# Linear attention ahead of two expert layers: output in natural layout with 128 moving columns, column-tiled own weights, scores last in a unit

## The chip, the cores and the metric

The program runs on one core of a Trainium2 chip, in one launch. The metric is the device time of one execution in microseconds (us), lower is better. The engines are called TensorE (PE; its weight loads are PEld), VectorE (DVE), ScalarE (ACT), GpSimd (POOL) and SyncE (SP, which issues most DMAs). Every engine executes its own instructions strictly in the order in which the program lists them.

## The reference

Three steps, each on the result of the one before, with 4 batches, 8 heads, 768 tokens and 48 numbers to a head (so 3072 rows of 384):

```python
for t in range(S):                       # attention, per batch and head
    cur = np.einsum('bhd,bhe->bhde', u[None] * kt, vt)
    y[:, :, t] = np.einsum('bhd,bhde->bhe', rt, state + cur)
    state = wt[:, :, :, None] * state + np.einsum('bhd,bhe->bhde', kt, vt)
# MoE 1: each row goes to the expert with the largest of 8 logits:
#   out = softmax weight * sigmoid(x @ w_output_gate)[e] * (relu(x @ w1[e]) @ w2[e])
# MoE 2: noisy logits, the two best experts of 8, weighted by a softmax over the two
```

## The kernel before

**Units.** The attention is cut into NU = 24 units: 128 tokens of one batch with all 8 heads, taken as 4 pairs of heads (HP = 4). Unit i is chunk i // 4 of batch i % 4, so the state that leaves unit i is needed by unit i + 4. Most tiles of a unit have 112 partitions (two heads of 48 at partitions 0 and 64) by 4 pairs by 128 tokens.

**What a unit needs.** `prep` (VectorE) clamps the decays w, scans them backwards to `g` and forwards to `cp`, and multiplies to `ke` = k*g and `R` = r*cp. `scores` (TensorE) multiplies ke with R into two PSUM banks; ScalarE copies them to `at` and GpSimd masks them (two `affine_select`). `keys` turns ke over, `kv` forms the unit's sum of outer products, `kv_add` (VectorE) adds the `carry` of the batch to `s0`, `carry_on` multiplies that by the next unit's whole decay, `advance` copies it to the block-diagonal `state`. `yout` adds, in one PSUM bank, state times R and v times at, with the heads' numbers on the partitions; ScalarE copies that out (`yT`), `ynat` turns it to natural layout (tokens on the partitions). The own term (r·u·k)v goes beside that: `ruk` forms p = r*k*u from a load of its own (GpSimd, two instructions), `bonus` sums it by head (VectorE, `s`) and multiplies v by it (GpSimd, `sv`). `rows_out` adds both to `x` and stores the 128 rows to `xrow` in memory. `xt` turns x over once more, `logits` multiplies it with the gates, and a `Route1` object does the routing of MoE 1: `choose` (8 small VectorE instructions), `rank` (TensorE), `place` (9 small VectorE instructions), `enter` (GpSimd scatters of 128 table entries).

**Order.** All queues are written by hand: the loop `for i in range(NU + 1)` lists for each engine the prep of unit i + 2, the scores of i, the kv and yout of i - 1, the ynat and x of i - 2 and the logits of i - 3. The routing is done in 12 groups of two units (`GROUPS`). Loads run three to four units ahead.

**Behind it.** When the rows are stored and routed, each expert's rows are gathered from `xrow`, and the two expert layers follow. `early` starts the first expert's work as filler before the last units are routed. PSUM has eight banks, and each name of `banks` is bound to one or two of them.

The own term passes from GpSimd to VectorE and back (p comes from `ruk`):

```python
s = wk.tile([C, H], F32, name="s")
nc.vector.tensor_reduce(s, t["p"].rearrange("p (h d) -> p h d", h=H), AX.X, OP.add)
sv = t["sv"] = wk.tile([C, H, D], F32, name="sv", bufs=3)
nc.gpsimd.tensor_tensor(sv, t["v"].rearrange("p (h d) -> p h d", h=H), bc(s, D), OP.mult)
```

Of the kernel before, what the change touches and what calls it, by code (L numbers as in the profile page):

```python
# [21 lines left out]
C = 128  # L22
# [10 lines left out]
MID = 2  # L33
FA, FB = 3, 1
EG = 6
FILL = (0, 1, 0, 0, 2)
NT = N + 128
W_MIN, W_MAX = 0.625, 1.25
TS = 16
# [14 lines left out]
GROUPS = [(i, 2) for i in range(0, NU, 2)]  # L54
# [11 lines left out]
def rwkv_moe_kernel(ctx, tc, r, k, v, w, rT, kT, wT, rkv, u, g1, a1, a2, g2, noise, b1, b2, out):  # L66
# [4 lines left out]
    psum = ctx.enter_context(tc.tile_pool(name="psum", bufs=1, space=PSUM))  # L71
# [50 lines left out]
    def banks(**plan):  # L122

        turns = {n: itertools.cycle(b) for n, b in plan.items()}
        return lambda name: psum.tile([128, 512], F32, name="b" + next(turns[name]))
# [370 lines left out]
    with ExitStack() as c2:  # L496
        ac = c2.enter_context(tc.tile_pool(name="ac", bufs=1))
# [5 lines left out]
        NS = HP * (C + 1)  # L503

        def flat(x):
            return x.rearrange("p a b -> p (a b)")

        def load(i):
            t = T.setdefault(i, {})
            for nm, src in (("w", wT), ("k", kT), ("r", rT)):  # L510
                t[nm] = ld.tile([PP, HP, C], F32, name=nm + "T")
                nc.sync.dma_start(t[nm], src[i])

        def load_rows(i):
            t = T.setdefault(i, {})
            t["rk"] = ld.tile([C, 2, DM], F32, name="rk")
            nc.sync.dma_start(t["rk"], rkv[i, :, 0:2])
            t["v"] = ld.tile([C, DM], F32, name="v", bufs=5)
            nc.sync.dma_start(t["v"], rkv[i, :, 2])

        bank = banks(sp0="0", sp1="1", kp="23", pp="4", yp="5", xp="6", lp="7")

        def quads(t, n=128):
            return t[:, 0:HP * n].rearrange("p (a b) -> p a b", a=HP)
# [4 lines left out]
        nc.vector.memset(sind, 0.0)  # L529
        nc.vector.memset(sind[:, :, C:C + 1], 1.0)  # L530
        clamped, start = [], []
        for i in range(2):
            t = ac.tile([PP, NS + 1], F32, name=f"clamped{i}")
            nc.vector.memset(t[:, ::C + 1], 0.0)
            clamped.append(t)
# [6 lines left out]
        ub = ac.tile([C, DM], F32, name="ub")  # L542
        nc.sync.dma_start(ub, rows(u, 0, [[0, C], [1, DM]]))
# [5 lines left out]
        state, carry = [], []  # L549
        for b in range(B):  # L550
            t = ac.tile([PP, HP, PP], F32, name=f"state{b}")
            nc.gpsimd.memset(t, 0.0)
            state.append(t)
            carry.append(ac.tile([PP, HP, D], F32, name=f"carry{b}"))
# [43 lines left out]
        def prep(i):  # L598
            t = T[i]
            v = nc.vector  # L600
            wc = clamped[i % 2]
            v.tensor_scalar(wc[:, 1:NS + 1].rearrange("p (a b) -> p a b", a=HP)[:, :, 0:C], t["w"],
                            W_MIN, W_MAX, OP.max, OP.min)
            yield
            g = wk.tile([PP, HP, C + 1], F32, name="g")
            v.tensor_tensor_scan(flat(g)[:, ::-1], wc[:, NS:0:-1], flat(sind)[:, ::-1], 0.0, OP.mult, OP.add)
# [6 lines left out]
            we = t["we"] = wk.tile([PP, HP], F32, name="we", bufs=6)  # L613
            v.tensor_copy(we, g[:, :, 0])
# [4 lines left out]
            R = t["R"] = wk.tile([PP, HP, C], F32, name="R", bufs=4)  # L619
# [10 lines left out]
        def bonus(i):  # L630
            t = T[i]
            s = wk.tile([C, H], F32, name="s")
            nc.vector.tensor_reduce(s, t["p"].rearrange("p (h d) -> p h d", h=H), AX.X, OP.add)
            sv = t["sv"] = wk.tile([C, H, D], F32, name="sv", bufs=3)
            nc.gpsimd.tensor_tensor(sv, t["v"].rearrange("p (h d) -> p h d", h=H), bc(s, D), OP.mult)

        def guard(i):
            w = T[i]["w"]
# [18 lines left out]
        def keys(i):  # L657
            t = T[i]
            kp = quads(bank("kp"))
            for pr in range(HP):  # L660
                nc.tensor.transpose(kp[:, pr, 0:PP], t["ke"][:, pr, :], ident[:PP, :PP])
            t["kk"] = wk.tile([C, HP, PP], F32, name="kk")
            nc.scalar.copy(t["kk"], kp[:, :, 0:PP])

        def kv(i):
            t = T[i]
            if i < NU - B:
                pp = t["pp"] = quads(bank("pp")[:PP], D)
                for pr in range(HP):
                    for r0, r1, c0 in ((0, 64, 0), (64, PP, D)):  # L670
                        nc.tensor.matmul(pp[r0:r1, pr, :], t["kk"][:, pr, r0:r1],
                                         t["v"][:, pr * 96 + c0:pr * 96 + c0 + D], start=True, stop=True)

        def kv_add(i):
            t = T[i]
            if i < NU - B:
                t["s0"] = wk.tile([PP, HP, D], F32, name="s0", bufs=4)
                if i < B:
                    nc.scalar.copy(t["s0"], t["pp"])
                else:  # L680
                    nc.vector.tensor_tensor(t["s0"], t["pp"], carry[i % B], OP.add)

        def carry_on(i):
            if i < NU - B:
                nc.vector.tensor_tensor(carry[i % B], T[i]["s0"], bc(T[i + B]["we"], D), OP.mult)

        def advance(i):
            if i < NU - B:
                for r0, r1, c0 in ((0, 64, 0), (64, PP, 64)):
                    nc.scalar.copy(state[i % B][r0:r1, :, c0:c0 + D], carry[i % B][r0:r1])  # L690

        def yout(i, prs=range(HP)):
            t = T[i]
            c, b = divmod(i, B)
            if prs[0] == 0:
                t["yp"] = quads(bank("yp")[:PP])
            yp = t["yp"]
            for pr in prs:
                if c:
                    nc.tensor.matmul(yp[:, pr, :], state[b][:, pr, :], t["R"][:, pr, :], start=True, stop=False)  # L700
                for hh in range(2):
                    h = 2 * pr + hh
                    m = 64 if hh == 0 else D
                    nc.tensor.matmul(yp[64 * hh:64 * hh + m, pr, :], t["v"][:, h * D:h * D + m], t["at"][:, hh, pr, :],
                                     start=(c == 0), stop=True)
            if prs[-1] == HP - 1:
                t["yT"] = wk.tile([PP, HP, C], F32, name="yT")
                nc.scalar.copy(t["yT"], yp)

        def ynat(i):  # L710
            t = T[i]
            yn = t["yn"] = quads(bank("kp"))
            for pr in range(HP):
                nc.tensor.transpose(yn[:, pr, 0:PP], t["yT"][:, pr, :], ident[:PP, :PP])

        def rows_out(i):
# [3 lines left out]
            nc.vector.tensor_tensor(x.rearrange("p (h d) -> p h d", h=H),  # L720
                                    t["yn"].rearrange("p a (h d) -> p (a h) d", h=2)[:, :, 0:D], t["sv"], OP.add)
# [5 lines left out]
        def xt(i):  # L727
            t = T[i]
            xp = quads(bank("xp"))[:, 0:KD]
            for k in range(KD):  # L730
# [93 lines left out]
        for _ in prep(1):  # L824
            pass
# [619 lines left out]
```

## Time and profile before

| | us |
|---|---|
| three runs: lowest, median, highest | 984.24, 985.2, 986.06 |
| the profiled execution, and its span | 983.54, 982.0 |
| busy: TensorE, VectorE, ScalarE, GpSimd | 894.6, 570.9, 421.6, 485.8 |
| first and last store of x | 34.1, 241.9 |
| mean granted TensorE clock, as a share of full speed | 0.945 |

The span is what the trace covers. The attention fills the first quarter of it and the expert layers the rest, so the busy shares of the whole span mix stages with different limits.

### The profile page before, as it was taken

The numbers are of one execution on the slowest core, as the hardware profiler recorded it, in microseconds if no ns is written. First come the engines' busy times: TensorE is split into PE (matmuls) and PEld (weight loads), VectorE is DVE, ScalarE is ACT, GpSimd is POOL, SyncE is SP. The second block draws the span as 40 slices with busy tenths as digits, with TensorE's granted clock in tenths as the row PEclk, the third lists the DMA queues.
The fourth block names the chain that finished last, engine by engine and source line by source line (L and its number), as shares of the span: only waits on it lengthen the run. The fifth ranks groups of instructions, "written<-read, shape, count | busy, mean of one in ns | idle before, by whom it ended". The sixth has DMA issues, their size and how long they took to land. (4 is left out here: it accounts for less than half of the span.)

```text
span 982.0 us, 16326 instructions
## 1 busy us (share of the span) xinstructions
PE 894.6 (91%) x5916; PEld 783.9 (80%) x5916; DVE 570.9 (58%) x1257; ACT 421.6 (43%) x929; POOL 485.8 (49%) x633
## 2 busy tenths in 40 slices
PE   7686777879779999999989899999999999999996
PEld 4464555656778899999977788989899898989995
DVE  7999999996345466556655156335361725434320
ACT  4555555455144445554544144333342524333320
POOL 4766776765242588659856443241423324151202
PEclk7888788698889999999999999999999999999998
DMA  9967566531355657666641454543444444444203
GB/s 237 230 215 211 141 164 184 130 93 56 84 148 154 164 125 169 185 166 177 124 153 25 111 141 119 121 96 89 78 138 75 122 98 98 91 105 110 35 9 41
DMA packets 86220, 123.02 MB, mean 125 GB/s; under 512 B 25986, under 2 KB 58255, under 8 KB 86120
## 3 DMA queue, kind: packets, MB, share of 16 engines
q1 hardware_dynamic: 60968, 90.50, 32.6%
q0 software_dynamic: 25152, 31.27, 17.3%
q8 instruction: 52, 0.85, 0.4%
q14 instruction: 48, 0.39, 0.2%
HBM read 96.60 MB, written 25.78 MB: 125 GB/s over the span
## 5 line engine op out<-in xcount | busy, mean ns | idle before, releaser
L108 POOL DMA_INDIRECT out<-yo,ent x54 | 84.9, 1573 | 274.7 <-ACT yo L1336 222.5
L177 PE MATMUL b<-xhi,w1h 128*128 128x512 f32 (+8 forms) x384 | 133.1, 347 | 0.0
L178 PE MATMUL b<-xlo,w1h 128*128 128x512 f32 (+8 forms) x384 | 132.2, 344 | 0.0
L179 PE MATMUL b<-xhi,w1l 128*128 128x512 f32 (+8 forms) x384 | 132.2, 344 | 0.0
L1080 DVE TENSOR_TENSOR xlo<-b,xhi 128x512 fp32r<-128x512 f32 (+8 forms) x48 | 27.1, 570 | 155.0 <-ACT xhi L1079 155.0
L1336 ACT ACTIVATE yo<-b,ent 128x384 f32<-128x384 f32 (+1 forms) x48 | 27.9, 581 | 166.4 <-issue 128.2
L108 POOL DMA_INDIRECT tab<-en,si x60 | 80.1, 1334 | 19.6 <-issue 14.6
L1323 PE MATMUL b<-w2h,hah 128*128 128x384 f32 x256 | 88.7, 346 | 0.4 <-PEq L1271 0.4
L1325 PE MATMUL b<-w2h,hal 128*128 128x384 f32 x256 | 86.9, 340 | 0.0
L1324 PE MATMUL b<-w2l,hah 128*128 128x384 f32 x256 | 86.7, 339 | 0.0
L177 PEld LDWEIGHTS b<-xhi,w1h 128*128 128x128 f32 x384 | 72.3, 188 | 11.8 <-issue 3.1
L177 PE MATMUL b<-hh,w2h 128*128 128x224 f32 (+7 forms) x216 | 74.9, 347 | 5.3 <-PEq L948 5.3
L178 PEld LDWEIGHTS b<-xlo,w1h 128*128 128x128 f32 x384 | 72.4, 189 | 8.7 <-DVE xlo L1080 0.2
L179 PEld LDWEIGHTS b<-xhi,w1l 128*128 128x128 f32 x384 | 72.3, 188 | 8.6
L177 PE MATMUL b<-xh,w1h 128*128 128x224 f32 (+7 forms) x216 | 75.5, 350 | 0.2 <-ACT xh L1126 0.2
L1089 DVE SCALAR_TENSOR_TENSOR hal<-b,hah 128x512 fp32r<-128x512 f32 x64 | 44.1, 691 | 52.3 <-ACT hah L1088 52.2
L165 DVE TENSOR_TENSOR w1l<-raw,w1h 128x512 fp32r<-128x512 f32 x92 | 61.7, 685 | 19.8 <-ACT w1h L164 19.3
L178 PE MATMUL b<-xl,w1h 128*128 128x224 f32 (+7 forms) x216 | 72.7, 337 | 0.1
L178 PE MATMUL b<-hl,w2h 128*128 128x224 f32 (+7 forms) x216 | 72.8, 337 | 0.0
L179 PE MATMUL b<-hh,w2l 128*128 128x224 f32 (+7 forms) x216 | 72.7, 337 | 0.0
L179 PE MATMUL b<-xh,w1l 128*128 128x224 f32 (+7 forms) x216 | 72.5, 336 | 0.0
L1137 DVE SCALAR_TENSOR_TENSOR hl<-b,hh 128x224 fp32r<-128x224 f32 (+7 forms) x64 | 35.8, 559 | 60.6 <-ACT hh L1136 60.5
(224 smaller groups left out, 2332.8 us busy)
## 6 DMA issues: line engine op xcount, KB each, us to landing
raw<-in_a SPq DMA_DIRECT2D x32, 768.0 KB, 5.9
raw<-in_b SPq DMA_DIRECT2D x30, 768.0 KB, 4.9
rk<-in_rkv SPq DMA_DIRECT2D x24, 384.0 KB, 5.2
wT<-in_wT SPq DMA_DIRECT2D x24, 224.0 KB, 4.9
kT<-in_kT SPq DMA_DIRECT2D x24, 224.0 KB, 6.0
rT<-in_rT SPq DMA_DIRECT2D x24, 224.0 KB, 5.2
v<-in_rkv SPq DMA_DIRECT2D x24, 192.0 KB, 6.7
xrow<-x SPq DMA_DIRECT2D x24, 192.0 KB, 1.9
```

The costliest lines, as they stand in the source:

```text
L108: st = nc.gpsimd.indirect_dma_start(out=table, out_offset=bass.IndirectOffsetOnAxis(ap=idx, axis=0), in_=src, in_offset=None, bounds_check ...
L165: eng.tensor_tensor(c, a, b.bitcast(F32), OP.subtract)
L177: nc.tensor.matmul(ps, st[0], mv[0], start=start, stop=False)
L178: nc.tensor.matmul(ps, st[0], mv[1], start=False, stop=False)
L179: nc.tensor.matmul(ps, st[1], mv[0], start=False, stop=stop)
L1080: nc.vector.tensor_tensor(t["lo"][:, k], p[:, 0:n], t["hi"][:, k].bitcast(F32), OP.subtract)
L1089: nc.vector.scalar_tensor_tensor(l, p[:, 0:n], 0.0, h.bitcast(F32), OP.max, OP.subtract)
L1137: nc.vector.scalar_tensor_tensor(l, p[:, c], 0.0, h.bitcast(F32), OP.max, OP.subtract)
L1323: nc.tensor.matmul(parts[0], h[:, f, sl], wh, start=(f == 0), stop=False)
L1324: nc.tensor.matmul(parts[0], h[:, f, sl], wl, start=False, stop=False)
L1325: nc.tensor.matmul(parts[0], l[:, f, sl], wh, start=False, stop=(f == NF - 1))
L1336: nc.scalar.activation(o, y, AF.Copy, scale=wgt2[:q, e, j:j + 1])
```

## The change

The output of a unit is formed in natural layout at once: the masked scores and R are now the stationary operands, and v (128 columns, of which 48 are used) and the carry (96 columns) are the moving ones, into a tile of two PSUM banks (`b45`). `ynat`, `yT`, the block-diagonal `state` and `advance` go. The own weights are formed from a product q = r*k in the layout of `prep` and four matmuls with u, each on 32 columns of the array, into the same bank as the turned x; one ScalarE copy takes both out, and a matmul with 8 columns turns them into `own`. `sv` is now VectorE's, straight from PSUM. The clamp goes: w is loaded into one of three `decay` tiles, and the backward scan takes the larger of the product and G_MIN. The load of r and k in natural layout goes. The carry is added in PSUM by a matmul with the identity, and ScalarE copies `s0` out. `keys` is left out for the last four units. In the loop prep is one unit ahead, x belongs to unit i - 1 and the logits to i - 2; the scores come last but for keys in a unit's TensorE order. Routing has groups of four units for the first 16 and of two for the rest (8 groups), `rank` comes one iteration after `choose`.

```diff
-GROUPS = [(i, 2) for i in range(0, NU, 2)]
+GROUPS = [(i, 4) for i in range(0, 16, 4)] + [(i, 2) for i in range(16, NU, 2)]
...
+        for i in range(3):
+            t = ac.tile([PP, NS + 1], F32, name=f"decay{i}")
...
         def prep(i):
...
-            v.tensor_scalar(wc[:, 1:NS + 1].rearrange("p (a b) -> p a b", a=HP)[:, :, 0:C], t["w"],
-                            W_MIN, W_MAX, OP.max, OP.min)
...
-            v.tensor_tensor_scan(flat(g)[:, ::-1], wc[:, NS:0:-1], flat(sind)[:, ::-1], 0.0, OP.mult, OP.add)
+            v.tensor_tensor_scan(flat(g)[:, ::-1], wc[:, NS:0:-1], flat(sind)[:, ::-1], 0.0, OP.mult, OP.max)
...
-            we = t["we"] = wk.tile([PP, HP], F32, name="we", bufs=6)
-            v.tensor_copy(we, g[:, :, 0])
+            yield
+            q = t["q"] = wk.tile([PP, HP, C], F32, name="q", bufs=3)
+            v.tensor_tensor(q, t["r"], t["k"], OP.mult)
...
-        def ruk(i):
-            t = T[i]
-            p = t["p"] = wk.tile([C, DM], F32, name="p")
-            eng = nc.gpsimd if i < EARLY + 3 else nc.vector
-            eng.tensor_tensor(p, t["rk"][:, 0], t["rk"][:, 1], OP.mult)
-            nc.gpsimd.tensor_tensor(p, p, ub, OP.mult)
...
+                if i >= B:
+                    nc.tensor.matmul(p[:, 0:HP * D], ident[:PP, :PP], carry[i % B].rearrange("p a d -> p (a d)"),
+                                     start=True, stop=False, skip_group_check=True)
...
+        def own(i):
+
             t = T[i]
...
+            t["own"] = bank("kp")[:C, 0:H]
+            nc.tensor.matmul(t["own"], t["oT"], ident.rearrange("p (a b) -> p a b", a=HP)[:, :, 0:2],
+                             start=True, stop=True)
+
+        def bonus(i):
+            t = T[i]
+            sv = t["sv"] = wk.tile([C, H, D], F32, name="sv", bufs=2)
+            nc.vector.tensor_tensor(sv, t["v"].rearrange("p (h d) -> p h d", h=H), bc(t["own"], D), OP.mult)
...
+                        nc.tensor.matmul(y[:, hh, pr, 0:2 * D], t["R"][r0:r0 + D, pr, :],
+                                         wide[b][r0:r0 + D, pr:pr + 2, :].rearrange("p a d -> p (a d)"),
+                                         start=(pr == 0), stop=False, skip_group_check=True)
...
+                    n = min(128, DM - h * D)
+                    nc.tensor.matmul(y[:, hh, pr, 0:n], t["at"][:, hh, pr, :], t["v"][:, h * D:h * D + n],
+                                     start=(c == 0 and pr == 0), stop=True, skip_group_check=True)
...
+                for pr in range(HP):
+                    nc.tensor.matmul(xp[32 * pr:32 * pr + 32, KD, :], ub[:, pr, :], T[j]["q"][:, pr, :],
+                                     start=True, stop=True)
...
+            if on[1] or on[2]:
+                xt(i - 2 if on[2] else None, i - 1 if on[1] else None)
+            if on[1]:
+                kv(i - 1)
+                yout(i - 1)
+                own(i - 1)
+            if ranked:
+                ranked.rank(bank("pp"))
+            if on[2]:
+                logits(i - 2)
             if on[0]:
                 scores(i)
...
+            if on[3]:
+                carry_on(i - 3)
+            if on[1]:
+                bonus(i - 1)
+                rows_out(i - 1)
+            take(choose, 9)
```

VectorE's order in one unit of the middle of the attention, before (numbers in names of carries and clamped tiles are buffers):

```order
L609 TENSOR_TENSOR ke<-kT,g 112x512
L681 TENSOR_TENSOR s_1144<-b_1128,carry_177 112x192
L633 TENSOR_REDUCE s<-p 128x8
L720 TENSOR_TENSOR x<-b_1123,sv 128x384
L612 RECIPROCAL start_142<-g 112x4
L614 COPY we<-g 112x4
L617 SCALAR_TENSOR_TENSOR cp<-clamped_138,start_142 112x516
L620 TENSOR_TENSOR R<-rT,cp 112x512
```

And the same engine in a unit of the changed kernel, from one prep to the store:

```order
L614 SCALAR_TENSOR_TENSOR g<-decay_125,sind 112x516
L617 TENSOR_TENSOR ke<-kT,g 112x512
L620 RECIPROCAL start_147<-g 112x4
L623 TENSOR_TENSOR q<-rT,kT 112x512
L626 SCALAR_TENSOR_TENSOR cp<-decay_125,start_147 112x516
L629 TENSOR_TENSOR R<-rT,cp 112x512
L692 TENSOR_TENSOR carry_165<-s_759,g 112x192
L688 TENSOR_TENSOR sv<-v,b_1018 128x384
L723 TENSOR_TENSOR x<-b_1001,sv 128x2x4x48
```

The sum s, the copy we and the sum with the carry (s<-b,carry) are gone; q and sv have come, and x stands behind the whole prep.

GpSimd's order in two units of the middle before (at is the masked scores, tab the routing table):

```order
L627 TENSOR_TENSOR p<-rk 128x384
L628 TENSOR_TENSOR p<-p,ub 128x384
L654 AFFINE_SELECT at<-at 128x512 x2
L635 TENSOR_TENSOR sv<-v,s 128x384
L107 MEMSET spacer 1x1
L108 DMA tab_69<-ent,slot 25600x2
```

And in the changed kernel (w2l is a part of a weight being split for MoE 1, which both kernels do there):

```order
L649 AFFINE_SELECT at<-at 128x512 x2
L164 TENSOR_TENSOR w2l_98<-raw,w2h_97 128x512
L106 MEMSET spacer 1x1
L107 DMA tab_66<-ent,slot 25600x2
L106 MEMSET spacer 1x1
L107 DMA tab_66<-ent,slot 25600x2
```

Of three products and two masks in a unit the masks are left; two scatters stand in one unit where one stood.

TensorE's order in a unit of the changed kernel, from the turning of x to keys (b is a PSUM bank; L682 is `own`, L191 the logits):

```order
L735 MATMUL b_1432<-ident,x 128x128 x3
L738 MATMUL b_1432<-q,ub 32x128 x4
L668 MATMUL b_1442<-carry_167,ident 112x192
...
L704 MATMUL b_1454<-carry_167,R 128x96 x8
L711 MATMUL b_1454<-v,at 128x128 x6
...
L682 MATMUL b_1471<-ident,xT 128x8
L191 MATMUL b_1228<-xT,g1s 32x128 x3
...
L657 MATMUL b_1491<-ident,ke 128x112 x4
```

Before, the carry's and the scores' matmuls of a unit's output alternated, with the logits between their halves:

```order
L700 MATMUL b_1416<-R,state_169 112x128
L704 MATMUL b_1416<-at,v 64x128
L704 MATMUL b_1416<-at,v 48x128
L192 MATMUL b_1294<-xT,g1s 32x128 x3
L700 MATMUL b_1416<-R,state_169 112x128
```

The first number of a shape is now 128, the tokens, and the second 128 or 96, the columns that move.

## Rows read from the trace of the kernel before

**Rows 1.** Windows by stage: busy us (x instructions) by engine, clock, DMA share, GB/s.

```profile
25.00:225.00 200.00, 152.12 (x1466) 113.53 (x1462) 197.58 (x381) 109.05 (x270) 141.17 (x178) 0.81 0.62 168
225.00:242.00 17.00, 16.10 (x149) 10.87 (x147) 9.92 (x34) 7.67 (x20) 11.85 (x18) 0.97 0.18 57
300.00:982.00 682.00, 663.82 (x3852) 606.98 (x3850) 319.68 (x728) 274.98 (x567) 301.77 (x390) 0.99 0.47 111
```

**Rows 2.** Tile xrow, the stores of x: min/median/max ns, first and last start.

```profile
L723 SPq DMA_DIRECT2D xrow<-x x24: 332/347/382, 34.1 to 241.9; - x24
```

**Rows 3.** Groups by source line, columns as in rows 2, then the shapes.

```profile
L606 DVE TENSOR_TENSOR_SCAN g<-clamped,sind x24: 1218/1226/1914, 4.7 to 217.3; 112x516 f32<-112x516 f32 x24
L620 DVE TENSOR_TENSOR R<-rT,cp x24: 691/694/1344, 8.0 to 222.3; 112x512 f32<-112x512 f32 x24
L602 DVE TENSOR_SCALAR clamped<-wT x24: 372/574/1497, 4.0 to 216.9; 112x512 f32<-112x512 f32 x24
L633 DVE TENSOR_REDUCE s<-p x24: 532/543/547, 25.8 to 236.4; 128x8 f32<-128x384 f32 x24
L685 DVE TENSOR_TENSOR carry<-s,we x20: 348/1146/2442, 37.4 to 225.2; 112x192 f32<-112x192 f32 x20
L720 DVE TENSOR_TENSOR x<-b,sv x24: 546/548/558, 33.5 to 241.3; 128x384 f32<-128x384 f32 x24
L635 POOL TENSOR_TENSOR sv<-v,s x24: 822/829/841, 26.4 to 238.8; 128x384 f32<-128x384 f32 x24
L654 POOL TENSOR_SCALAR_AFFINE_SELECT at<-at x48: 624/764/1650, 13.5 to 231.8; 128x512 f32<-128x512 f32 x48
```

**Rows 4.** Timeline of one unit: start, duration, engine, line, operation.

```profile
142.76 1.06 ACT L653 COPY at<-b 128x512 f32<-128x512 f32 x2
143.65 1.00 POOL L628 TENSOR_TENSOR p<-p,ub 128x384 f32<-128x384 f32 x1
143.72 0.96 DVE L282 TENSOR_TENSOR sl<-rk,base 128x16 f32<-128x16 f32 x1
143.95 0.68 PE L671 MATMUL b<-v,kk 128*64 128x48 f32 x16
```

**Rows 5.** Timeline of the last group's routing on VectorE.

```profile
246.12 0.26 DVE L202 TENSOR_REDUCE L<-b 128x32 f32<-128x96 f32 x1
247.66 0.17 DVE L264 TENSOR_REDUCE o<-og 128x2 f32<-128x16 f32 x1
248.94 0.17 DVE L282 TENSOR_TENSOR sl<-rk,base 128x16 f32<-128x16 f32 x1
249.78 0.17 DVE L302 RECIPROCAL ent<-se 128x2 f32<-128x2 f32 x1
```

**Rows 6.** Timeline of TensorE, late in the attention: idle before and its releaser in brackets.

```profile
208.83 1.16 PE L649 MATMUL b<-R,ke 48*128 48x128 f32 x16
211.04 0.52 PE L731 MATMUL b<-ident,x 128*128 128x128 f32 x3 [1.05 <-DVE start L612]
211.40 0.55 PE L714 MATMUL b<-ident,yT 112*128 112x112 f32 x4
212.17 0.38 PE L700 MATMUL b<-R,state 112*112 112x128 f32 x2
212.48 0.43 PE L704 MATMUL b<-at,v 128*64 128x128 f32 x4
214.01 0.42 PE L192 MATMUL b<-xT,g1s 128*32 128x128 f32 x6 [0.33 <-DVE L L202]
220.75 0.19 PE L221 MATMUL b<-qr,ones 128*128 128x8 bf16 x2 [4.79 <-DVE x L720]
220.93 2.08 PE L649 MATMUL b<-R,ke 48*128 48x128 f32 x16
```

**Rows 7.** Timeline of VectorE at the start, the prep of units 1 and 2.

```profile
11.22 0.53 DVE L602 TENSOR_SCALAR clamped<-wT 112x512 f32<-112x512 f32 x1 [1.87 <-DMA wT<-in_wT]
22.12 0.69 DVE L620 TENSOR_TENSOR R<-rT,cp 112x512 f32<-112x512 f32 x1
```

More of the change, by code (lines that the diff above doesn't have):

```diff
@@ L528, in rwkv_moe_kernel @@
         sind = ac.tile([PP, HP, C + 1], F32, name="sind")
-        nc.vector.memset(sind, 0.0)
+        nc.vector.memset(sind, G_MIN)
         nc.vector.memset(sind[:, :, C:C + 1], 1.0)
[L531 to L535, printed above, removed]
+        start = []
         for i in range(2):
@@ L548, in rwkv_moe_kernel @@
             nc.sync.dma_start(t[:, :, 0:2 * E], g)
-        state, carry = [], []
-        for b in range(B):
-            t = ac.tile([PP, HP, PP], F32, name=f"state{b}")
+        wide = [ac.tile([PP, HP + 1, D], F32, name=f"carry{b}") for b in range(B)]
+        carry = [t[:, 0:HP] for t in wide]
+        for t in wide:
             nc.gpsimd.memset(t, 0.0)
-            state.append(t)
-            carry.append(ac.tile([PP, HP, D], F32, name=f"carry{b}"))
         load(2)
@@ L671, in kv @@
                         nc.tensor.matmul(pp[r0:r1, pr, :], t["kk"][:, pr, r0:r1],
-                                         t["v"][:, pr * 96 + c0:pr * 96 + c0 + D], start=True, stop=True)
-        def kv_add(i):
-            t = T[i]
[L676 to L681, printed above, removed]
+                                         t["v"][:, pr * 96 + c0:pr * 96 + c0 + D],
@@ L683, in carry_on @@
         def carry_on(i):
             if i < NU - B:
[L685 to L692, printed above, removed]
+                nc.vector.tensor_tensor(carry[i % B], T[i]["s0"], bc(T[i + B]["g"][:, :, 0], D), OP.mult)
@@ L822, in rwkv_moe_kernel @@
             pass
-        ruk(0)
-        for _ in prep(1):
-            pass
-        load(3)
         guard(0)
-        guard(1)
         none = iter(())
@@ L872, in rwkv_moe_kernel @@
-            if on[1]:
-                bonus(i - 1)
-            if on[2]:
-                rows_out(i - 2)
-            if on[3]:
-                advance(i - 3)
-            if on[1]:
-                yout(i - 1, range(MID))
-            if on[3]:
-                logits(i - 3)
-            if on[1]:
-                yout(i - 1, range(MID, HP))
-            if rt:
-                rt.rank(bank("kp"))
-            turn(i - 3)
-            take(pre, 9)
-            if i >= EARLY + 4 and i + 1 < NU:
-                ruk(i + 1)
@@ L890, in rwkv_moe_kernel @@
-            if i - 5 in RT and i != EARLY + 5:
-                waiting += [(RT[i - 5], j) for j in range(RT[i - 5].nj)]
-            if i == EARLY + 4:
+            if early_rt:
+                rt.rank(bank("xp"))
+            if ranked:
+                take(ranked.place(), 9)
+                waiting += [(ranked, j) for j in range(ranked.nj)]
+            if 8 <= i < 20:
+                w_split(0, 0, *divmod(i - 8, 3), nc.gpsimd if i % 3 else nc.vector)
+            if early_rt:
                 take(rt.place(), 9)
@@ L915, in rwkv_moe_kernel @@
         flag(wk, 0, p[0:1, 0:1], 0.0)
-        r1, r2 = NU - 3, NU - 1
-        xt(NU - 2)
         take(fill)
-        ynat(NU - 1)
-        rows_out(NU - 1)
-        choose = RT[r1].choose()
-        for _ in range(3):
-            take(choose, 2)
-            take(fill)
-        take(choose, 9)
-        logits(NU - 2)
-        RT[r1].exps()
+        xt(r2)
+        take(RT[r1].place(), 9)
+        for j in range(RT[r1].nj):
+            RT[r1].enter(j, "tab1")
+        take(fill, 3)
         take(fill, FILL[0])
-        xt(NU - 1)
+        logits(r2)
         take(fill, FILL[1])
-        RT[r1].rank(bank("kp"))
-        take(fill, FILL[2])
-        logits(NU - 1)
-        take(fill, FILL[3])
-        take(RT[r1].place(), 9)
-        for j in range(2):
-            RT[r1].enter(j, "tab1")
-        turn(NU - 1)
+        turn(r2)
         take(RT[r2].choose(), 9)
         RT[r2].exps()
-        take(fill, FILL[4])
+        take(fill, FILL[2])
         RT[r2].rank(bank("kp"))
@@ L944, in rwkv_moe_kernel @@
         rank_experts(wk, 0)
-        for j in range(2):
+        for j in range(RT[r2].nj):
             RT[r2].enter(j, "tab1")
```

189 lines of the change are left out of this document (92 added, 97 removed).

## The prediction

> **What bounds the kernel now.** I read first the windows by stage [rows 1]. From 25 to 225 us VectorE is busy 197.58 of 200 us, TensorE 152.12, GpSimd 141.17; the granted TensorE clock is 0.81. From 300 us on TensorE is busy 663.82 of 682 us at 0.99. So there are two stages with two limits, VectorE in the attention and TensorE in the expert layers, and the diff touches only the first. The experts' work follows on the routing of the last unit's rows, so the change is worth as much as the last store of x moves. Next I read when x is stored [rows 2]: 24 times, first at 34.1, last at 241.9. That is 207.8 us for 23 units, 9.03 us each.
>
> What fills VectorE's 9.03 us? I added the shortest time that each of its instructions took [rows 3]: clamp 0.372; two scans at 1.218; ke and R at 0.691; carry 0.348 and the sum s0 like it; s 0.532; x 0.546. That is 5.96 us a unit, 137 us in 23 units (the reciprocal and the copy `we`, with 4 numbers a partition, are left out, as are the few units without s0 or carry, which about make up for them). Two more shares are known. Routing, from the one group that the trace shows undisturbed [rows 5]: choose from 246.12 to 247.83, place from 248.94 to 249.95, 1.71 + 1.01 = 2.7 us; ten groups fall inside, 27 us. Idle time near the end: 17 - 9.92 = 7 us [rows 1]. The rest is 207.8 - 137 - 27 - 7 = 37 us, in which VectorE counts as busy but its instructions last longer than their shortest: carry has a median of 1.146, the clamp 0.574 [rows 3]. The timeline shows with what [rows 4]: `sl`, 16 numbers a partition, starts at 143.72 and ends at 144.68, just behind GpSimd's product p (143.65 to 144.65); the same line took 0.17 where GpSimd was quiet [rows 5]. VectorE stands still behind GpSimd's elementwise work. That work in the 23 units is 44 us for two products a unit (22 units with both, 1.0 each) [rows 4], 23 x 0.83 = 19 for sv and 46 to 48 masks at 0.624, 30 [rows 3]: some 93. So 37 us of stalls are 39% of it.
>
> **VectorE's own work.** Removed: clamp 0.37, s 0.53, s0 0.35, together 1.25. Added: q, shaped like R, 0.69, and sv, shaped like x, 0.55, together 1.24. The two cancel, and 6.0 a unit stays. The gain does not come from there.
>
> **GpSimd.** Both products and sv leave: 63 of the 93 us. The masks stay, 30 us. At 39% they cost VectorE 12 us, 0.5 a unit, for 6.5 in all. Bounds: nothing, and the full 30 us if each mask stops VectorE all the way. The rule that bears on it stands in the Trainium skill, page "SBUF — State Buffer", section "Who interferes with whom": a VectorE instruction with two SBUF inputs and a GpSimd instruction that reads SBUF exclude each other for the whole instruction. By that rule the price would be nearer the upper bound, for all but sv and x, which read PSUM; the stretched `sl` agrees with it, the total of 39% with a part of it.
>
> **Routing.** The instructions are counted per group, and at these sizes their time is that of an instruction: 0.17 with 128x8 or 128x16 alike [rows 5]. Groups of four cost the same 2.7. Inside the 23 intervals lie six choose and six place instead of ten of each. Choose adds 1.7 to one iteration of the loop, place 1.0 to the next one; in one iteration (the sixth group's early one) both fall together.
>
> **TensorE.** At the upper clock, from start to start where the next group follows at once [rows 6]: xt 0.36 (211.04 to 211.40); the logits 0.35 (0.42 with their end); scores 1.16; keys as the four turns of `ynat`, 0.4; kv 0.68 [rows 4]. New: the four own-weight matmuls are eight passes like the six of the logits, 0.47; identity times carry two passes like L700, 0.31 (212.17 to 212.48); R with the carry 16 passes on half the rows as in the scores, 1.16; own 0.2; rank and turn 0.2 on average. The unknown is at times v: 16 passes with 128 stationary and 128 moving columns, which before were 64 or 48 stationary. The row with the narrow weights took 0.43 for four passes, that with 112 took 0.38 for two, so 0.11 to 0.19 a pass, 1.7 to 3.0 in all; near the scores, whose weights also have 128 columns and take 0.07 a pass, it would be 1.2. I take 2.0. Gone are ynat and the old output. The sum is 7.3 us a unit (bounds 6.5 to 8.3), where VectorE needs 6.5.
>
> **The ring through both.** xt on TensorE waits for x of the unit before, sv on VectorE waits for `own` of this unit. From xt to own TensorE has 0.36 + 0.47 + 0.68 + 0.31 + 1.16 + 2.0 + 0.2 = 5.2; meanwhile VectorE does its prep and carry, 4.9 with stalls; then sv and x, 1.1, and some 0.3 of handovers: 6.6. That is under TensorE's 7.3, because logits and scores run while VectorE does sv and x. The masks' way, from scores over ScalarE's copies (1.06 for two [rows 4]) and GpSimd (1.25) to the next output, has 3.4 us of cover on TensorE (keys, xt, own weights, kv, carry) and costs nothing; without that cover it would cost up to 2.3 a unit.
>
> **Sum of the loop.** Each iteration takes the longer of 7.3 and VectorE's 6.5 with its routing: 5 with choose at 8.2, 5 with place at 7.5, one with both at 9.2, 12 at 7.3. That is 41.0 + 37.5 + 9.2 + 87.6 = 175, and 2 for waits between queues: 177, 7.7 a unit.
>
> **The start.** Before, three preps stand ahead of x(0): that of unit 1 begins at 11.2 and that of unit 2 ends at 22.8, 5.8 each [rows 7], and x(0) comes at 34.1 behind a part of a fourth and the turns of its output. After, two preps stand ahead of it. They would end at 17.0; q twice is 1.4, sv and x 1.1, and the masks and the output of unit 0 some 2.5: the first store at 22, between 20 (they overlap) and 25 (loads are late, as the 1.87 us of waiting for wT show) [rows 7].
>
> **Costed at nothing.** Loads stand two iterations (15 us) ahead instead of three or four, and 384 KB a unit less are fetched; DMA share was 0.62 [rows 1]. The three decay tiles are written by DMA only when the scan of three units before has passed. ScalarE was busy 109 of 200 us [rows 1]; it loses yT and state and gains s0. The new PSUM pool behind the attention makes the first MoE turn wait for ScalarE's last copies: up to 1 us, which I add.
>
> **Sum.** x(23) at 22 + 177 = 199 instead of 241.9: -43. With +1 behind it, -42. The profiled execution's 983.54 becomes about 941.5. It lies 1.7 under the median of the runs, 985.2, so the median becomes 943.
>
> **The rivals.** Faster still: at times v runs like the scores (1.2) and masks stall nobody. VectorE at 6.0 and TensorE at 6.5: 12 x 6.6 for the ring, 5 x 7.7, 5 x 7.0 and 8.7 give 161 us; with the first store at 20, 181, that is -60: 925. For it speaks that the narrow `carry` has a minimum of 0.348; against it the median of the masks, 0.764, over their own shortest, 0.624 [rows 3]: the two engines do meet. Chance 0.12.
>
> TensorE as the bound: the wide weights at L700's rate or the masks come late, 8.3 us a unit; a fifth of the time at the lower clock (below) would give as much, 7.3 x (0.8 + 0.2 x 1.79) = 8.5. 22 x 8.3 and 9.2 are 192, with 2 for waits 194: x(23) at 216, 960. For it speaks that L700, with 112 stationary columns, is the nearest row by width; against, that the scores are quicker with more. Chance 0.2.
>
> Masks at full price: 30 us of stalls instead of 12, 0.8 more a unit on VectorE. Iterations of 7.3, 9.0, 8.3 and 10.0 give 87.6 + 45 + 41.5 + 10 = 184, with waits 186: x(23) at 208, 952; if the masks wait for VectorE in their turn, and TensorE for them by 0.4 a unit, 217 and 961. For it speaks `sl`, stopped all the way [rows 4]; against, that 37 of 93 us were lost and not 93. Chance 0.08.
>
> Slower than before: TensorE's clock stays at its lower level of 1.2 GHz. The scores took 1.16 at one level and 2.08 at the other, the latter behind 4.79 us of waiting for x [rows 6]. The new ring makes TensorE wait on VectorE in each unit. At the low level a unit would take 7.3 x 2.08 / 1.16 = 13.1; all 23 at it, 301: x(23) at 323, some 1067. It decides from (241.9 - 1 - 22) / 23 = 9.5 us a unit, that is with 38% of the time at the low level, a granted clock of 0.81: just that of before [rows 1]. What the stage grants is therefore the point. Against the rival: that 0.81 goes with a TensorE that is busy for 76% of the stage, and in stretches in which it is busy for 95% or more the clock is 0.97 and 0.99 [rows 1]; here TensorE bounds most units, and the slower it goes, the less it waits. After a wait of 1.05 us xt still ran at the upper level [rows 6]. Chance 0.05.
>
> That the change does nothing to the time, since a wait of loads or of the store's queue takes over what VectorE gives back: DMA's share of 0.62 before [rows 1] leaves no room for it: 0.02. My forecast has 0.53.
>
> **How the numbers follow.** The predicted time is the likeliest case, 943, with its own range of 930 to 955 (start 20 to 25, masks 0 to 30 us in part, at times v 1.7 to 2.5). The range for 8 in 10 takes in most of the faster case and the two that gain less: 923 to 967. Faster by over 0.2% (2 us, about what a measurement of this kernel can tell from no change): 0.53 + 0.12 + 0.2 + 0.08, less 0.01 that TensorE's case passes the point, 0.92; same 0.02; slower 0.06.
>
> **What would show it.** The stores of x: first near 22, last near 199, 7.7 apart, with longer steps at the routing. VectorE's carry near 0.35 and sl near 0.17 at the median if GpSimd was the cause; TensorE busy over 90% of the attention at a granted clock above 0.85; the 16 passes of at times v at 0.12 each; the stage from the branch on as long as before. The forecast is wrong if carry stays stretched (masks lock as much as the products did), if TensorE waits for at or own by over 1 us in each unit, or if its clock falls under 0.7 in the attention.

## The result, and the profile after

The changed kernel takes 944.85 us (median of four runs, 941.78 to 950.27) beside 985.35 for the kernel before; the ratio is 0.9596, 95% interval 0.9549 to 0.9642. The forecast was 943, its range 923 to 967. The profiled execution took 950.27 us with a span of 948.7, the longest of the four. In three of the experiments below (two products, 48 columns, scores first) some executions lay well above the fastest of the same kernel; the ratios leave those out.

The windows of the changed kernel from the first to the last store of x, and from the expert stage on, in the columns of [rows 1]; then its stores of x, to hold against [rows 2]:

```profile
20.40:202.50 182.10, 171.69 (x1959) 141.00 (x1957) 156.28 (x301) 94.72 (x232) 79.58 (x133) 0.92 0.55 146
264.40:948.70 684.30, 665.25 (x3853) 608.01 (x3851) 319.26 (x728) 275.15 (x567) 301.23 (x390) 0.99 0.47 110
L725 SPq DMA_DIRECT2D xrow<-x x24: 332/362/376, 20.4 to 202.5; - x24
```

The last store of x came 39.4 us earlier: 13.7 from the start (34.1 to 20.4) and 25.7 from the 23 units, 7.92 us each instead of 9.03. The expert stage is as long as before. The bound has changed sides: TensorE is busy 171.69 of 182.10 us, VectorE 156.28; before, VectorE was all but full.

Groups of VectorE and GpSimd by source line, columns as in [rows 3]:

```profile
L617 DVE TENSOR_TENSOR ke<-kT,g x24: 681/749/1583, 6.1 to 185.8; 112x512 f32<-112x512 f32 x24
L688 DVE TENSOR_TENSOR sv<-v,b x24: 540/547/556, 19.2 to 201.4; 128x384 f32<-128x384 f32 x24
L692 DVE TENSOR_TENSOR carry<-s,g x20: 344/351/785, 34.2 to 189.6; 112x192 f32<-112x192 f32 x20
L649 POOL TENSOR_SCALAR_AFFINE_SELECT at<-at x48: 626/636/1609, 12.2 to 198.5; 128x512 f32<-128x512 f32 x48
```

Carry's median went from 1.146 [rows 3] to near its shortest, 0.344; sv, now on VectorE, takes 0.540 to 0.556. Most of the stretching that is left sits in ke, q and the two scans. Beside a mask ke takes about 1.0 us, and beside GpSimd's part of a weight split (w1l or w2l) 1.58 (timeline, columns as in [rows 4]):

```profile
30.19 1.67 POOL L649 TENSOR_SCALAR_AFFINE_SELECT at<-at 128x512 f32<-128x512 f32 x2 [5.21 <-ACT at L648]
30.36 1.00 DVE L617 TENSOR_TENSOR ke<-kT,g 112x512 f32<-112x512 f32 x1
125.39 1.38 POOL L164 TENSOR_TENSOR w2l<-raw,w2h 128x512 fp32r<-128x512 f32 x1 [1.32 <-ACT w2h L163]
125.74 1.58 DVE L617 TENSOR_TENSOR ke<-kT,g 112x512 f32<-112x512 f32 x1
```

One unit on TensorE, from scores to scores (timeline, columns as in [rows 6]):

```profile
54.72 1.16 PE L644 MATMUL b<-R,ke 48*128 48x128 f32 x16
55.81 0.60 PE L657 MATMUL b<-ident,ke 112*128 112x112 f32 x4
56.25 0.49 PE L735 MATMUL b<-ident,x 128*128 128x128 f32 x3
56.67 0.43 PE L738 MATMUL b<-q,ub 112*32 112x128 f32 x8
57.03 0.58 PE L668 MATMUL b<-carry,ident 112*112 112x192 f32 x2
57.54 0.67 PE L672 MATMUL b<-v,kk 128*64 128x48 f32 x16
58.13 1.14 PE L704 MATMUL b<-carry,R 48*128 48x96 f32 x16
59.20 1.99 PE L711 MATMUL b<-v,at 128*128 128x128 f32 x16
61.02 0.35 PE L682 MATMUL b<-ident,xT 128*128 128x8 f32 x2
61.85 1.16 PE L644 MATMUL b<-R,ke 48*128 48x128 f32 x16
94.17 0.60 PE L657 MATMUL b<-ident,ke 112*128 112x112 f32 x4 [0.97 <-DVE sv L688]
100.06 3.65 PE L711 MATMUL b<-v,at 128*128 128x128 f32 x16
162.98 1.01 PE L657 MATMUL b<-ident,ke 112*128 112x112 f32 x4 [2.24 <-DVE sv L688]
```

The unit from 54.72 to 61.85 took 7.13 us without a gap to speak of; the term that no row of before could show, at times v, took 1.99. Behind the wait of 0.97 at 94 the same 16 passes took 3.65: that is TensorE's lower level, 1.2 GHz of 2.4, with a granted clock of 0.52 from 94 to 108 us. Five units ran so for a part or all of their time, with x stored 9.9 to 11.0 us after the one before it instead of some 7.4. Together that is about 14 us, the waits themselves included; these units stand behind the waits at 94 and 163.

### The profile page after: what moved, and what is told of

Its sections match the earlier page's. It is cut to its first block, busy times and chain, and to the rows that moved or that the text cites. A ratio compares the mean times of both kernels' runs of the same rounds, so it can differ in the third digit from the quotient of the medians.

```text
span 948.7 us, 16623 instructions
## 1 busy us (share of the span) xinstructions
PE 901.2 (95%) x6244; PEld 804.4 (85%) x6244; DVE 516.7 (54%) x1146; ACT 395.0 (42%) x862; POOL 404.4 (43%) x562
## 5 line engine op out<-in xcount | busy, mean ns | idle before, releaser
L649 POOL TENSOR_SCALAR_AFFINE_SELECT at<-at 128x512 f32<-128x512 f32 x48 | 39.3, 841 | 103.5 <-ACT at L648 103.5
```

Of the source, the lines that this page charges most:

```text
L649: nc.gpsimd.affine_select(at[:, hh], at[:, hh], [[0, HP], [1, C]], OP.is_gt, 0.0, base=0, channel_multiplier=-1)
```

## The experiments

Each was timed against the kernel before on its own chip, so ratios are compared. On the chip of four of them (two products, fills, the first run with groups of two, 48 columns) the kernel before took 1005.9. The run with fills, whose stores of x ended at 196.0 there, lost its time behind them: in the first expert stage TensorE waited 15.0 us in two waits for ScalarE's copies of gathered rows (`xh`), where the changed kernel's two traces have 0.2 us at most. What held these copies up was not shown.

**The changed kernel again**, as a reference beside the runs without products, with scores first and with own apart.

> The changed kernel once more, as the reference for the others here: 0.9596 of the kernel before, 0.955 to 0.964; last store of x between 194 and 204, by how many units run at the lower TensorE clock (some 3 us each).

Measured: 941.22, ratio 0.9574 (0.9546 to 0.9603), stores of x from 21.1 to 204.1.

**The kernel before without GpSimd's products.** k and u are left out of the own term.

```diff
-            eng.tensor_tensor(p, t["rk"][:, 0], t["rk"][:, 1], OP.mult)
-            nc.gpsimd.tensor_tensor(p, p, ub, OP.mult)
+            p = t["p"] = t["rk"][:, 0]
```

> The kernel before without GpSimd's two products a unit (and without VectorE's one in the last units): s is the sum of r alone, so k and u are left out of the own term; all else as before, sv on GpSimd too. Theory (VectorE stands still during 39% of GpSimd's reading): 44 of the 93 us go, so 17 of 37 us of stalls, and the time falls by 12 to 20 us, a ratio of 0.980 to 0.988; carry's median falls from 1.15 to under 0.6. If the products caused nearly all of the stalls: 30 to 37 us, 0.963 to 0.97. Rival (the stalls have another cause): 1.00, 0.003 either way.

Measured: 949.44, ratio 0.9674 (0.9641 to 0.9706), 33 us less than the kernel before. The store of x(0) starts at 37.7 in this run, but x(0) is ready at 30.35: the store stands behind two loads (rk and v) in SyncE's queue. The window therefore goes from the time at which x(0) is ready to the last store. Then that run's carry and its stores:

```profile
30.35:202.50 172.15, 156.21 (x1567) 113.34 (x1567) 163.33 (x397) 111.16 (x282) 105.48 (x125) 0.87 0.65 196
L682 DVE TENSOR_TENSOR carry<-s,we x20: 347/350/1271, 32.8 to 186.9; 112x192 f32<-112x192 f32 x20
L720 SPq DMA_DIRECT2D xrow<-x x24: 332/422/1432, 37.7 to 202.5; - x24
```

The same window of the kernel before, and GpSimd's products in it (count, busy us, mean ns):

```profile
34.05:241.90 207.85, 165.22 (x1567) 122.01 (x1567) 198.60 (x402) 112.47 (x280) 145.48 (x164) 0.83 0.57 155
L628 POOL TENSOR_TENSOR p<-p,ub 128x384 f32<-128x384 f32 x21 | 22.4, 1067 | 4.3 <-DVE sl L282 2.4 <-DVE p L627 0.5
L627 POOL TENSOR_TENSOR p<-rk 128x384 f32<-128x384 f32 x17 | 21.2, 1245 | 0.3
```

VectorE is busy 35.3 us less, of which 4 x 0.55 are its own products in the last four units: 33 us for 44 us of GpSimd's products. That is three quarters, not the four tenths that I had spread evenly over all of GpSimd's work. What stayed in this run still cost VectorE time. Summed over VectorE's lines in these windows, the time above each line's shortest is some 60 us in the kernel before, 26 here and 21 in the changed kernel (without the copy `we`, which has a median of 0.47 us in both runs that have it). With `we` it is 33 us here, and by what ran beside, an estimate, about 13 of them go with the masks, 10 with sv and 9 with the weight splits. The 23 units take 172 us, less than the changed kernel's 182.1: the rebuilt form by itself, with q and its wider output, is not quicker per unit in these two executions than the old one rid of its products. What it has over that run is its earlier start, by 10 us.

**Two products, or two fills, put into the changed kernel.**

```diff
+        def products(i):
+            v = T[i]["v"]
+            p = wk.tile([C, DM], F32, name="p")
+            nc.gpsimd.tensor_tensor(p, v, v, OP.mult)
+            nc.gpsimd.tensor_tensor(p, p, v, OP.mult)
...
+            if i + 1 < NU:
+                products(i + 1)
```

The run with fills has `nc.gpsimd.memset(p, 0.0)` and `nc.gpsimd.memset(p, 1.0)` in the place of the two products.

> The changed kernel with two GpSimd products of 128x384 numbers from SBUF added to each unit at the place where the old kernel had its two (v times v, then that times v; nobody reads the result). Theory (VectorE stands still behind GpSimd's reads of SBUF, at about 39% of their time): 46 products of 1.0 us bring back 18 us of stalls, 0.8 a unit; carry's median rises from 0.35 to 0.5 or more, ke's and R's too. VectorE goes from 6.5 to 7.3 a unit, about level with TensorE, so the time rises by 5 to 18 us, to 950 to 963. If each product stops VectorE for its whole length, VectorE needs 8.5 and the time rises by 28 us or more, to 973. Rival (the long carry and clamp of the kernel before had another cause, and the gain came from fewer steps): carry's median stays under 0.4 and the time stays at 945, 4 us either way.

> The same as the run with two products, but with two GpSimd fills of the same 128x384 tile, which write and read nothing. If it is GpSimd's reading of SBUF that stops VectorE, carry's median stays at 0.35 and the time at 945, 4 us either way. If any work on GpSimd does, the run is like that with the products, less in so far as the fills are shorter: 948 to 958.

Measured: with products 997.8, ratio 0.9874 (0.9787 to 0.996); with fills 965.55, ratio 0.9588 (0.9534 to 0.9643), which is the changed kernel's. Windows over the stores of x, VectorE's carry and the fills or products, of the run with products:

```profile
21.70:227.40 205.70, 182.94 (x1956) 151.07 (x1954) 177.86 (x301) 95.06 (x230) 130.82 (x176) 0.86 0.46 129
L692 DVE TENSOR_TENSOR carry<-s,g x20: 343/568/1421, 36.0 to 207.6; 112x192 f32<-112x192 f32 x20
L719 POOL TENSOR_TENSOR p<-p,v x23: 997/1327/1816, 15.7 to 212.9; 128x384 f32<-128x384 f32 x23
```

and of the run with fills:

```profile
20.40:196.00 175.60, 164.10 (x1959) 134.60 (x1957) 155.90 (x301) 94.79 (x232) 99.09 (x177) 0.96 0.55 153
L692 DVE TENSOR_TENSOR carry<-s,g x20: 345/352/785, 34.2 to 183.1; 112x192 f32<-112x192 f32 x20
L717 POOL MEMSET p<- x23: 412/418/481, 14.6 to 188.7; 128x384 f32 x23
```

Both runs add one pair of instructions a unit at GpSimd. The pair that reads stretches carry and costs VectorE 22 us (177.86 against 155.90), while the pair that only writes costs nothing (155.90 against the changed kernel's 156.28). The fills are also shorter, 19 us in all against some 50; at the products' price for their length they would have cost 8 us. So it is the reading that stops VectorE. The time rose more than forecast, about 29 us by the two ratios and the chip's 1006, though the first ratio is known only to 9 us either way. VectorE makes TensorE wait longer (17.3 us in 12 waits of keys, against 7.1 in 8 with fills), and the clock fell to 0.86. The Trainium skill, page "SBUF — State Buffer", section "Who interferes with whom", has both halves: a VectorE instruction with two SBUF inputs meets GpSimd's reads, not its writes. These two runs agree. By the page the lock is held for a whole instruction; 33 us for 44 in the kernel before comes near that. It is 22 us for some 50 here (23 x 0.86 and 23 x 1.33), where the products themselves grow longer (the second has a shortest of 1.00), which says that GpSimd also does a part of the waiting.

**Groups of two units throughout.**

```diff
-GROUPS = [(i, 4) for i in range(0, 16, 4)] + [(i, 2) for i in range(16, NU, 2)]
+GROUPS = [(i, 2) for i in range(0, NU, 2)]
```

> The changed kernel with routing groups of two units throughout (12 groups again, not 8); everything else as changed. Theory (TensorE is now the longer of the two in plain units, so VectorE's routing costs only what stands out over it): four more choose iterations at 0.9 and four more place iterations at 0.2 are 4 us; with a further stretch at the lower TensorE clock, seen behind each long wait of keys for sv, up to 15: 949 to 960. Rival 1 (VectorE still bounds): the whole 4 x 2.7 = 11 us, 956, with TensorE's waits longer in every unit. Rival 2 (routing is all hidden): 945, 3 us either way.

> The run with routing groups of two units throughout, once more, since there the last store of x came only 4.6 us later than in the run with fills, and the time was 11.3 us longer. If the further 7 us came from that chip's first expert stage (its matmuls waited 15.6 us for weights), the ratio to the kernel before is now 0.960 to 0.968, 3 to 8 us over the changed kernel's 0.957 to 0.960. If groups of two cost that much in themselves, it is 0.97 or more again.

Measured: 976.86, ratio 0.9714 (0.9648 to 0.9781), 11 us over the run with fills on that chip; and on another chip 948.43, ratio 0.9645 (0.9608 to 0.9683). The second is 5 to 7 us over the changed kernel's two ratios. TensorE's waits of keys, of that second run:

```profile
PE b L657 <- DVE sv L688: 13.5, 15, 2.4
```

and of the changed kernel (us in total, times, longest):

```profile
PE b L657 <- DVE sv L688: 6.2, 8, 2.2
```

So the routing's four groups are worth 5 to 7 us, what stands out over TensorE's time, and not 11. The larger figure of the first chip did not come back. There the last store of x came 4.6 us after that of the run with fills (200.6 against 196.0), and the rest of the 11 us lies behind it; what caused that rest was not shown.

**48 moving columns.**

```diff
-                    n = min(128, DM - h * D)
+                    n = D
```

> The changed kernel with 48 moving columns of v in each matmul with the masked scores instead of 128 (the other 80 are never used). Theory (a pass with 128 stationary columns is set by loading them, 0.116 us a pass as in the changed kernel's 1.99 us for 16): the 16 passes stay between 1.8 and 2.0 and the time at 945, 4 us either way. Rival 1 (a pass is set by its moving columns): 16 passes take 0.8 to 1.2, TensorE's unit falls from 7.1 to 6.1, the ring through VectorE bounds at 6.5, and the time falls to 925 to 935. Rival 2 (fewer columns in motion make the granted clock fall): passes as long at the upper clock, but a granted clock under 0.88 in the attention instead of 0.91, and 950 to 965.

Measured: four runs of 980.68, 989.74, 1010.77 and 1011.58, too wide for a ratio; the kernel before had 1002.4 to 1011.7. The two lower ones are 1.6 and 2.5% over the run with fills on the same chip. Timeline and windows over the stores of x:

```profile
55.31 1.99 PE L711 MATMUL b<-v,at 128*128 128x48 f32 x16
20.50:218.60 198.10, 188.70 (x1959) 154.96 (x1957) 155.80 (x301) 94.94 (x232) 81.00 (x133) 0.82 0.49 134
```

The 16 passes take 1.99 us with 48 columns as with 128: the columns do not set the time of a pass with 128 stationary ones. But the granted clock of the stage was 0.82 in this execution (989.7) instead of 0.92 or 0.96, and x(23) came at 218.6. The columns that nobody reads cost nothing in a pass. That leaving them out is what lowered the clock is not shown: it is one execution, and among the others, with 128 columns, the clock of the stage goes from 0.91 to 0.96 as well.

**Scores at the head of the iteration.**

```diff
+            if on[0]:
+                scores(i)
             if on[1] or on[2]:
                 xt(i - 2 if on[2] else None, i - 1 if on[1] else None)
...
                 logits(i - 2)
-            if on[0]:
-                scores(i)
```

> The changed kernel with the scores of a unit at the head of TensorE's order in each iteration, before xt, instead of behind the logits. Theory (the ring: x, xt, kv, output, own, sv, x bounds a unit as soon as something more stands in it; scores last fill the time in which VectorE does sv and x): the scores' 1.16 us now lie in the ring, 6.6 becomes 7.7 or more against TensorE's own 7.1, keys wait for sv in nearly every unit by 0.6 us, and with the lower clock behind such waits the time rises by 10 to 35 us against the changed kernel, a ratio to the kernel before of 0.97 to 0.995. Rival (TensorE is busy all through and its order is free): 0.9596, 0.004 either way.

Measured: 963.05, ratio 0.9777 (0.9727 to 0.9828), 20 us over the reference on that chip. Timeline of the profiled execution (970.73) at the upper clock, and of the scores of the same units in the changed kernel:

```profile
43.58 1.16 PE L644 MATMUL b<-R,ke 48*128 48x128 f32 x16
58.83 1.16 PE L644 MATMUL b<-R,ke 48*128 48x128 f32 x16
66.22 0.60 PE L657 MATMUL b<-ident,ke 112*128 112x112 f32 x4 [0.58 <-DVE sv L688]
66.76 1.16 PE L644 MATMUL b<-R,ke 48*128 48x128 f32 x16
90.96 1.16 PE L644 MATMUL b<-R,ke 48*128 48x128 f32 x16
```

```profile
47.45 1.16 PE L644 MATMUL b<-R,ke 48*128 48x128 f32 x16
92.04 1.16 PE L644 MATMUL b<-R,ke 48*128 48x128 f32 x16
```

With the same matmuls six units in a row take 7.90 us each at the upper clock (scores at 43.58 to 90.96), where the same six take 7.43 in the changed kernel (47.45 to 92.04), and keys wait for sv, 10.4 us in 14 waits of 0.30 and more. The ring through x, own and sv is there, as the prediction had it. At 0.47 us a unit it is about 11 of the 20 us; what the rest is made of was not shown, though in the profiled execution the clock of the stage was 0.82.

**Own in another bank.** Keys no longer wait for sv, and the own weights' matmuls stand ahead of the turning of x.

```diff
-            t["own"] = bank("kp")[:C, 0:H]
+            t["own"] = bank("pp")[:C, 0:H]
...
-            for k in range(k0, KD):
-                nc.tensor.transpose(xp[:, k, :], T[i]["x"][:, k * 128:(k + 1) * 128], ident)
...
+            for k in range(k0, KD):
+                nc.tensor.transpose(xp[:, k, :], T[i]["x"][:, k * 128:(k + 1) * 128], ident)
...
-                ranked.rank(bank("pp"))
+                ranked.rank(bank("xp"))
```

> The changed kernel with own in the PSUM bank of kv instead of that of keys (rank in the bank of xt), so that keys no longer wait until sv has read own, and with the four own-weight matmuls ahead of the turning of x, so that TensorE has 0.8 us more that doesn't wait for x. Theory (what is left to gain lies in TensorE's waits of about 1 us in the iterations with routing or a weight split on VectorE, and in the lower clock that follows them): keys' waits for sv, 6.2 us in 8, go; xt's wait for x grows by less; fewer units at the lower clock: 3 to 15 us less than the changed kernel, a ratio of 0.945 to 0.957. Rival (the wait only moves from keys to xt and the clock falls as before): 0.9596, 0.004 either way.

> The run with own apart once more, as the reference for the others here: 0.953 of the kernel before, 0.950 to 0.956.

Measured: 935.35, ratio 0.9528 (0.9497 to 0.9559), every run below every run of the reference beside it; and 936.56, ratio 0.951 (0.9467 to 0.9553). Windows over the stores of x, and what is left of the waits:

```profile
21.10:190.60 169.50, 157.29 (x1953) 130.90 (x1952) 154.10 (x301) 92.58 (x228) 76.19 (x131) 0.98 0.57 157
PE b L740 <- DVE x L723: 5.2, 7, 1.1
```

This beats both kernels, by 6 us in the medians on one chip (935.35 against 941.22). The total of the waits fell little (the wait moved from keys, 7.8 us in 9 in the reference, to xt, 5.2 in 7), but the clock went from 0.91 to 0.98 and x(23) from 204.1 to 190.6. The 13.5 us between these two stores are more than the medians' 6, since the profiled execution of the reference is the slowest of its five. The bank and the order were changed together, so which of them did it is not shown.

**Matmuls put into the waits.**

```diff
+            if i in (11, 19):
+                filler(1 if i == 11 else 3, "pp")
             if on[0]:
                 keys(i)
```

> The changed kernel with matmuls that nobody reads put into TensorE's two longest waits of keys for sv: one of 512 columns in iteration 11 (a wait of 0.96 us), three in iteration 19 (2.24 us), between scores and keys. Theory (TensorE drops to its lower clock because of these waits, for one to three units each): the granted clock stays at 1.00 from 90 to 110 and from 160 to 190 us, the five units of 10 us and more become units of 7.5 to 8.5, and the last store of x moves from 204 to between 188 and 197: 6 to 15 us less, a ratio of 0.942 to 0.952. Rival (the clock falls whatever TensorE does between the units): the same units run at the lower clock, and the time is the changed kernel's, 0.957 to 0.960, or up to 2 us more by the work added.

Measured: 938.03, ratio 0.9543 (0.9502 to 0.9584). Windows over the stores of x:

```profile
20.20:192.80 172.60, 163.15 (x1967) 132.33 (x1966) 155.67 (x301) 94.83 (x232) 79.68 (x133) 0.99 0.56 155
```

The granted clock of the stage was 0.99, and x(23) came 10 us earlier than in the changed kernel's profile, although TensorE had work added. The five units that were slow there took 9.5 us less, about half of it behind each of the two waits. For the wait at 94 the filler is not shown to be the cause. The run with fills at GpSimd left its waits of 1.05, 0.98 and 1.11 us as they were, and it too ran at 1.00 up to 158 us:

```profile
20.40:158.00 137.60, 128.88 (x1604) 104.97 (x1602) 127.98 (x223) 79.11 (x192) 76.08 (x136) 1.00 0.64 178
102.60 0.60 PE L657 MATMUL b<-ident,ke 112*128 112x112 f32 x4 [0.98 <-DVE sv L688]
```

For the second wait the filler is the likelier cause: left open it was 2.24 us in the changed kernel and in its repeat and 2.13 in the run with fills, and each time units at the lower clock stood behind it. A part of the wait only moved: TensorE now waits 2.08 us for the rank at 167, where it waited 0.71 at 175 in the changed kernel. The medians are only 3 to 5 us below the changed kernel's two by the ratios, and the intervals meet: the profiled execution (933.7) is the fastest of its five, that of the reference (945.4) the slowest of its own. So the gain of the filling cannot be told from nothing in the time.

**The same in the run with own apart**, at its longest wait (2.71 us, ahead of the rank of the sixth group):

```diff
             if early_rt:
+                filler(3)
                 rt.rank(bank("xp"))
```

> The run with own apart, with three such matmuls more in the early iteration in which TensorE waits 2.71 us for the choice of the sixth group (its rank follows in the same iteration). In the run with own apart the granted clock was 1.00 up to 150 us and fell behind that wait at 164. By the theory that waits bring the lower clock: the units behind it run at 1.00 and the time falls by 3 to 8 us against the run with own apart, a ratio of 0.944 to 0.950. Rival: no change, 0.953, 0.003 either way.

Measured: 938.67, ratio 0.9545 (0.9502 to 0.9588): no gain over the run with own apart beside it, 936.56. The clock did stay at 1.00 from 150 to 175, but x(23) came at 190.9 against 191.8. This wait is not worth filling.

## Why the prediction was right, step by step

The mechanism was right: GpSimd's products had stretched VectorE, and without them TensorE bounds the attention. That the median came within 2 us of the forecast is in part luck, because terms that were missed on both sides nearly cancel. The profiled execution, 950.27, lies 8.8 above the 941.5 that the sum gave for it.

**GpSimd stops VectorE: right in kind, its size wrong.** The step "So 37 us of stalls are 39% of it" is too low. Its 137 us count 23 units of prep, but only 19 or 20 of each prep instruction run between the first and the last store of x. They also add up whole durations, where one instruction's end overlaps the next one's start. The stretching was some 60 us, and the products alone cost three quarters of their length, 33 of 44 us. (The 44 came out although the window holds 17 and 21 products and not 22 of each, since they are longer than 1.0.) This did not harm the forecast, since the products and their stalls leave together and TensorE bounds what is left.

**The masks: about right, and hidden by the count.** The forecast gave them 12 us, and VectorE's busy time 137 + 16 + 12 = 165; it came out at 156. The masks are not what is missing. Two of the 23 preps stand ahead of the first store, some 9 us by their shortest times, and overlapping ends take more. Against that the changed kernel's VectorE is stretched by 21 us: by what ran beside, an estimate, about 10 go with the masks and 9 with eight weight splits on GpSimd (12.4 us), which the prediction did not price. "The gain does not come from there", said of VectorE's own work, holds; the largest part of it is the two products leaving.

**TensorE's unit: right.** Forecast 7.3, measured 7.13 at the upper clock; at times v 2.0 and 1.99, where 2.0 was a choice between 1.2 and 3.0.

**The clock: the term that was missing.** "Granted clock above 0.85" held with 0.92, but no time stood for it. Five slow units cost 14 us, where 2 us stood for all waits; in the run with two waits filled the same five took 9.5 us less. It stood only among the rivals, as a fifth of the time at the lower clock. The argument against it, that stretches in which TensorE is busy for 95% had 0.97 and more, does not hold: with 48 columns it was busy 188.70 of 198.10 us at 0.82. Against the slow units, the start came at 20.4 instead of 22, and three units near the start (6.3 to 6.5 us, two of them without a carry) and the last three (6.0 each, no keys) were shorter than 7.3: 182 us instead of 177.

**The ring: right.** Scores last keep it under TensorE's own time; put first, they cost 2%, about half of it in the ring itself.

**Routing: right, by one chip of two.** 5 to 7 us for four groups, near what the sum had (0.9 and 0.2 an iteration, 4.4), not their 11 us of instructions.

**Behind x(23): within its error.** 746 us to the end against 740 before in the two profiled executions; 739.6 in the reference. The 1 us of the forecast cannot be told from nothing.

## What to carry to other kernels

Before an engine's own work is counted, hold its shortest durations against its medians; where they differ, find what the other engine reads at that time: here a fill cost nothing, and a product three quarters of its length where VectorE was the bound. When two windows are compared, count what runs in them first: a prep more or less was 4 to 5 us here, and it first looked like a stall. When the bound moves to TensorE, look for the clock behind its waits: here that cost more than the waits themselves. A bank shared by two stages that have nothing to do with each other, together with the order of four matmuls, was worth 6 us. Keep what fills a wait of the other engine (here the scores) at the place of the wait.

## What was unexpected

The 16 passes with 128 stationary columns took 1.99 us whether 128 or 48 columns moved. And the clock did not answer to each wait alike: 0.97 and 2.24 us were followed by the lower level in the changed kernel, but its wait of 1.10 at 131 us, that of 0.98 in the run with fills, 1.11 in the reference and 1.10 in the run with own apart were not. What decides between them stays open.
